# Attention block: constants filled by plan, the opening's norms in other PSUM banks, a 16-bit root for Q's norm, and another set of tie-breaks

## The chip, the cores and the metric

The kernel runs on one NeuronCore of a Trainium2 chip. A run's time is device time in microseconds. The kernel before has a median of 359.07 us over three runs (359.01 to 359.48). Times inside a run come from one profiled execution and are counted from its first instruction. The engines are TensorE (PE, matmuls), VectorE (DVE), ScalarE (ACT), GpSimd (POOL) and SyncE (SP, which issues DMAs here; ACT and POOL issue some too).

## The reference

```python
B, S, D, H = 1, 2048, 448, 16
qkv = (x @ wqkv).reshape(B, S, 3, H, Dh).transpose(2, 0, 3, 1, 4)
q, k, v = qkv[0], qkv[1], qkv[2]
scores = einsum("bhqd,bhkd->bhqk", q, k) * (Dh ** -0.5)
p = softmax(scores)
o = einsum("bhqk,bhkd->bhqd", p, v)
return o.transpose(0, 2, 1, 3).reshape(B, S, D) @ wo
```

All of x, wqkv and wo are bfloat16. A head has 28 columns. There are 16 heads of 2048 x 2048 scores, so 67 million exponentials.

## The kernel before

**Tiling.** The heads form four groups of four. A head takes 32 rows of the 128 partitions (28 columns and four rows for constants). The queries form four chunks of 512, the keys 16 tiles of 128. A set is one group with one chunk; 16 sets run one behind the other. Inside a set each head meets 16 key tiles, and one head with one tile and 512 queries is a *half*: 1024 halves in all. The scores of a half are one matmul of 32 rows (line 798), which leaves 128 keys x 512 queries in a PSUM bank.

**Two ways for an exponential.** ACT takes two halves at once from a pair of banks, `a0` or `a1`, and writes `pt` (line 1001, `do_exp`). DVE takes one half from bank `d0` or `d1`, sometimes `m` (line 1016, `do_a`). It writes the score, shifted and clipped, as an int16, whose bits read as a bfloat16 stand for a power of two (the tile `I`). Four halves make a *chain*, one `I` tile of 128 x 2048. As that power of two is only piecewise linear, each chain is used three times: as it is, and with two shifts added to the integer (`SHIFT` 43 and 85), against V, and V scaled by two weights (`VS`, `VW`). The first shift is written by DVE into a tile `J1` (line 1114, `do_add`). The second is either a second DVE write, into `J2`, or for chains that begin early in a set (`own`, set in `d_more`) an accumulating DMA that POOL issues: it adds the tile `shift2`, a constant 85, to `I` in place once the unshifted `I` has been used (line 1074, `in_place`).

**Sums.** The product with V goes to bank `o` in groups of four matmuls, one for each head (line 1176). V has a column of ones, so a set's last rows are the sums. At a set's end DVE copies `o` to `o_sb`; SP moves the sums, DVE inverts them, SP stores the result to `scr` and spreads it as `rr`, and POOL multiplies (line 1228), into `xs` or `OTL`. The output projection (line 348, bank `m`) follows.

**A bound for the softmax.** Instead of the row maximum the scores carry a bound from the norms of Q and K. For the first group it is found in the opening: `k_first` squares each K block (ACT), sums the squares by a matmul (line 452) into a bank given by its argument `nbank`, and takes the maximum on DVE (line 457). `qn_first` does the same for the first Q chunk: a matmul into a bank, an approximate square root by integer arithmetic on the bits (line 534), and the product with the root of K's largest norm (line 539), called `su`. The first scores need `su`.

**The order of the work.** One function, `plan`, writes all instructions in the order that a small planner finds. It keeps a time for each engine, gives each piece of work a duration, a priority, what it needs and what it gives, and lets the engine that is free first choose. `best` picks the ready piece of the lowest priority number. For DVE and POOL a piece can be marked `port`: then it isn't begun while the other engine is in such a piece. `after_shared` makes a POOL instruction wait for the last such DVE instruction. Small random numbers in the costs (`shake`) break ties; the plan is tried for 24 seeds, and the one with the earliest planned end is written (lines 1460 and 1461). Every engine's queue is in order.

**Outside the plan** stand the opening's loads and fills, written ahead of it. On POOL these are, in order, the identity, the cleared weights and V tiles, 14 small DMAs with constant rows for QP (line 231), then `shift2` (line 257), the float copy of the identity `identf` (line 258) and `self_`. The planner takes POOL as free from 25.6 us on. `identf` is first used in the kernel's last microseconds.

**The end.** Behind the last set's product, the projection's first three groups for each of four tiles of 128 queries are done early where PE has room (`early_jobs`); what is left of them is written by `filler` between the last steps. Then the last group follows (`OTf`), the copies (lines 1440, 1442) and the stores.

The lines that choose the seed:

```python
d = Dry()
ends = {k: plan(d, d, d, d, d, d, k, True) for k in range(NSEED)}
seed = min(ends, key=lambda k: ends[k])
```

## Time and profile before

| what | value |
|---|---|
| median of three runs | 359.07 us |
| the profiled execution's own time | 360.29 us |
| its span, first to last instruction | 358.2 us |
| busy: PE, DVE, ACT, POOL | 94%, 92%, 94%, 32% of the span |
| mean granted PE clock | 1.000 |
| exponentials on ACT | 358, from 17.27 to 349.24 us |
| halves on DVE | 278 from d, 30 from m |
| J writes on DVE | 104 |
| accumulating DMAs | 50, of 512 KB |

A row of a group of instructions has line, engine, operation, out<-in, shapes and count; then busy time and the mean of one in ns; then the idle time of the engine before them, and what ended it. A row of the timeline begins with the start and the duration in us, and has in brackets the idle time ahead of it and what ended that. A row of the chain has start, duration and what ran. In DMA queue rows (SPq, POOLq) the duration is that of the issue. Idle time counts only where the engine is the one that others wait for.

### The profile page before, as it was taken

The page shows a single profiled execution, that of the slowest core. Times are in us where ns is not written, and L with a number is a line of the kernel's source. Part 1 is how long each engine was busy: PE and PEld are TensorE (multiplying, and loading weights), DVE is VectorE, ACT ScalarE, POOL GpSimd, SP SyncE. Part 2 cuts the span into 40 slices and gives each one's busy share as a digit, 9 for nine tenths or more (in the row PEclk, how much of TensorE's full clock was granted, in tenths as well). Part 3 has the DMA queues.
Part 4 walks back from the last instruction along what each step waited for, and adds up shares of the span by engine and source line. Part 5 has one row for each costly group of instructions (what it writes and reads, how often), then busy time and mean ns, then how long its engine had stood idle before and what let it go on. Part 6 is the DMA issues. An engine that isn't in the chain of part 4 may idle for free.

```text
span 358.2 us, 11057 instructions
## 1 busy us (share of the span) xinstructions
PE 338.0 (94%) x4474; PEld 110.3 (31%) x4474; DVE 329.4 (92%) x616; ACT 338.1 (94%) x370; POOL 115.3 (32%) x164
## 2 busy tenths in 40 slices
PE   8999999999999999999989999988899899999994
PEld 4333233332234332332222222222222322222232
DVE  7789989999999899998999999999999999999933
ACT  2689999999999999999999999999999999999991
POOL 8971252413503043432223535121414131130110
PEclk9999999999999999999999999999999999999999
DMA  9430146551746437094393916464585929395211
GB/s 208 105 97 15 25 95 131 119 112 36 147 98 120 91 61 150 10 191 89 86 186 77 193 34 136 94 139 102 104 165 97 198 62 203 90 185 120 66 33 54
DMA packets 29463, 38.73 MB, mean 108 GB/s; under 512 B 15108, under 2 KB 21092, under 8 KB 29412
## 3 DMA queue, kind: packets, MB, share of 16 engines
q0 software_dynamic: 7648, 26.25, 38.5%
q1 hardware_dynamic: 20516, 11.22, 12.2%
q8 instruction: 35, 0.57, 0.7%
q10 hardware_dynamic: 1248, 0.55, 0.6%
q14 instruction: 16, 0.13, 0.1%
HBM read 6.20 MB, written 1.96 MB: 23 GB/s over the span
## 4 chain that ended last, share of the span: by engine, by line
PE 45%; ACT 37%; issue 7%; DVE 6%; DMA 3%; POOL 0%; SPq 0%; POOLq 0%; ACTq 0%; DVEq 0%
ACT pt L1001 37%; PE a L798 17%; PE o L1176 13%; PE m L341 5%; PE m L348 5%; DVE I L1016 3%; DMA scr<-rec 2%; PE o L696 1%; DVE J L1114 1%; DVE kp L457 1%; DMA rr<-scr 1%; PE d L348 1%; PE d L798 1%; PE a L341 1%; DVE V L612 0%
## 5 line engine op out<-in xcount | busy, mean ns | idle before, releaser
L1001 ACT ACTIVATE pt<-a 128x1024 bf16<-128x1024 f32 x358 | 329.5, 1167 | 3.2 <-PE d L798 1.7
L1016 DVE TENSOR_SCALAR I<-d 128x512 int16<-128x512 f32 x278 | 181.4, 680 | 9.2 <-PE d L798 8.6
L798 PE MATMUL a<-QP,KA 32*128 32x512 bf16 (+1 forms) x708 | 138.2, 380 | 11.3 <-ACT pt L1001 10.3
L1176 PE MATMUL o<-pt,V 128*32 128x512 bf16 x716 | 102.7, 383 | 0.0
L798 PE MATMUL d<-QP,KA 32*128 32x512 bf16 x275 | 95.4, 384 | 0.8 <-DVE I L1016 0.8
L798 PEld LDWEIGHTS <-KA 32*128 32x128 bf16 (+1 forms) x1035 | 48.6, 91 | 145.4 <-issue 143.7
L1074 POOL DMA_DIRECT2D I<-shift x50 | 44.0, 941 | 99.9 <-PE o L1176 28.4
L1114 DVE TENSOR_SCALAR J<-I 128x2048 int16<-128x2048 int16 x104 | 72.9, 709 | 0.7
L1176 PE MATMUL o<-I,V 128*32 128x512 bf16 x308 | 60.0, 385 | 0.0
L1176 PE MATMUL o<-J,VS 128*32 128x512 bf16 x212 | 36.0, 383 | 0.0
L1176 PEld LDWEIGHTS <-V 128*32 128x32 bf16 x1024 | 26.8, 94 | 29.8 <-issue 29.1
L1176 PE MATMUL o<-J,VW 128*32 128x512 bf16 x204 | 31.3, 384 | 0.0
L1228 POOL TENSOR_TENSOR xs<-o_sb,rr 128x512 bf16<-128x512 f32 x12 | 15.9, 1323 | 44.3 <-DMA rr<-scr 21.9
L363 POOL TENSOR_TENSOR sq<-QA 128x512 bf16<-128x512 bf16 x15 | 17.2, 1146 | 23.9 <-DVE QA L503 18.2
L363 POOL TENSOR_TENSOR sq<-KA 128x512 bf16<-128x512 bf16 x12 | 13.4, 1117 | 24.4 <-DVE KA L381 13.8
L1016 DVE TENSOR_SCALAR I<-m 128x512 int16<-128x512 f32 x30 | 20.2, 675 | 0.1
L341 PE MATMUL m<-XT,WRAW 128*32 128x512 bf16 x216 | 18.3, 386 | 0.0
L1228 POOL TENSOR_TENSOR OTL<-o_sb,rr 128x512 bf16<-128x512 f32 x3 | 3.8, 1264 | 34.4 <-DMA rr<-scr 21.7
L1176 PE MATMUL o<-I,VW 128*32 128x512 bf16 x108 | 13.7, 385 | 0.0
L348 PE MATMUL m<-WRAW,XT 128*32 128x112 bf16 (+1 forms) x432 | 13.5, 231 | 0.0
L1176 PEld LDWEIGHTS <-VS 128*32 128x32 bf16 x304 | 10.1, 94 | 9.3 <-issue 8.7
L348 PE MATMUL m<-WO,xs 128*32 128x448 bf16 x156 | 12.7, 358 | 0.0
(133 smaller groups left out, 275.8 us busy)
## 6 DMA issues: line engine op xcount, KB each, us to landing
I<-shift POOLq DMA_DIRECT2D x50, 512.0 KB, 6.0
rr<-scr SPq DMA_DIRECT2D x60, 64.0 KB
QP<-QA SPq DMA_DIRECT2D x60, 28.0 KB
out_dram<-osb SPq DMA_DIRECT2D x12, 112.0 KB
WRAW<-in_wqkv_dram SPq DMA_DIRECT2D x3, 336.0 KB
QP<-su SPq DMA_DIRECT2D x32, 2.0 KB
WO<-in_wo_dram SPq DMA_DIRECT2D x16, 24.5 KB
den<-o_sb SPq DMA_DIRECT2D x15, 8.0 KB
```

The lines of the kernel that those rows point to most:

```text
L341: nc.tensor.matmul(out=ps[HP * i:HP * (i + 1), :], lhsT=w[:, cc, h * Dh:h * Dh + HP], rhs=xt(c, cc), start=(cc == 0), stop=(cc == CC - 1), ...
L348: nc.tensor.matmul(out=out[r, :], lhsT=lhsT[:, r], rhs=rhs, start=start, stop=stop, tile_position=(0, HP * i), **k)
L363: after_shared(nc.gpsimd.tensor_tensor(out=t[:], in0=src, in1=src, op=ALU.mult))
L457: nc.vector.reduce_max(out=held["kp"][:, sc:sc + 1], in_=held.pop(nkey), axis=AX.X)
L696: nc.tensor.matmul(out=warm[:], lhsT=zero[:, 0:P], rhs=zero[:], start=True, stop=True)
L798: nc.tensor.matmul(out=out_ap, lhsT=KAt[(g, j // XB)][r, (j % XB) * P:(j % XB + 1) * P], rhs=q[r, :], start=(n == 0), stop=(n == len(terms ...
L1001: nc.scalar.activation(out=pt[:], in_=ps[:], func=ACT.Exp, scale=LN2 / 128.0)
L1016: nc.vector.tensor_scalar(out=dst, in0=pd[:], scalar1=BIAS, scalar2=0.0, op0=ALU.add, op1=ALU.max)
L1074: after_shared(nc.gpsimd.dma_start(out=ch["I"][:, w], in_=shift2[:, w], accum_op=ALU.add))
L1114: cur["shared"] = nc.vector.tensor_scalar(out=r[:, w], in0=ch["I"][:, w], scalar1=float(SHIFT[k]), scalar2=None, op0=ALU.add)
L1176: nc.tensor.matmul(out=o[HP * i:HP * (i + 1), :], lhsT=v_of(e["k"], g, j)[:, HP * i:HP * (i + 1)], rhs=e["ap"], start=(SETMM[key] == 1), s ...
L1228: m = nc.gpsimd.tensor_tensor(out=otile(g, c), in0=st["o_sb"][:], in1=st["rr"][:], op=ALU.mult)
```

## The change

Six things are changed.

- The constants. The fill of the shift tile and the cast to `identf` leave POOL's unplanned opening and become planned pieces, marked `port`: the fill as soon as the second Q chunk is in SBUF, the cast behind the fills of `WO`. Both wait for DVE's last marked instruction.
- The banks of the opening's norms: K's four norms are in o, o, a0, o, where they were in o, a0, o, a0; Q's norm is in a0, where it was in o, and has priority 2.5 for 3.15.
- The root of Q's norm is written as 16 bits (the upper half of the float's bits, read as bfloat16), where it was 32 bits. `su` reads it.
- `J1` tiles are taken when they are written, from four buffers; they were taken at the chain's start, from five. `dve_ok` no longer asks for them.
- The path by which a whole chain's first shift was accumulated into J1 (`far`) is removed; its threshold had kept it unused. In its place stands a way to accumulate both shifts (`own2`), whose threshold of 999 keeps it unused too.
- The seeds are 70 to 93, where they were 0 to 23.

Since the planner decides, all else follows: the built program has 44 accumulating DMAs (50 before), 110 J writes (104), 34 halves from bank m and 274 from d, 12 groups of filling matmuls on zeros in the main part (18), and the same 358 exponentials on ACT. The diff, cut:

```diff
-    NJ = 5
-    FAR = 99
+    NJ = 4
+    OWN2 = 999
...
+    SEED0 = 70
     NSEED = 24
...
-    shift2 = const.tile([P, HG * QW], I16, name="shift2")
-    nc.gpsimd.memset(shift2[:].bitcast(I32), SHIFT[2] * 65537)
-    nc.gpsimd.tensor_copy(out=identf[:], in_=ident[:])
+    shifts = {v: const.tile([P, HG * QW], I16, name=f"shift{v}") for v in ...}
...
             def root():
-                held["nq"] = wk.tile([P, 2 * QW], BF16, name="pt", bufs=NPT)[:].bitcast(F32)
-                nc.vector.tensor_scalar(out=held["nq"].bitcast(I32), in0=held.pop("qn0").bitcast(I32), scalar1=0.5,
-                                        scalar2=float(127 << 22), op0=ALU.mult, op1=ALU.add)
+                held["nq"] = wk.tile([P, 2 * QW], BF16, name="pt", bufs=NPT)[:, 0:QW]
+                nc.vector.tensor_scalar(out=held["nq"].bitcast(I16), in0=held.pop("qn0").bitcast(I32), scalar1=0.5 ** 17,
+                                        scalar2=float(127 << 6), op0=ALU.mult, op1=ALU.add)
...
-            add("DVE", 0.34, scaled, need=["nq0", ("km", 0)], gives=[("QA", 0, 0), "QN00"], pri=pri)
+            add("DVE", 0.27, scaled, need=["nq0", ("km", 0)], gives=[("QA", 0, 0), "QN00"], pri=pri)
...
+        def fill_shift(v):
+            after_shared(nc.gpsimd.memset(shifts[v][:].bitcast(I32), v * 65537))
+
+        def copy_ident():
+            after_shared(nc.gpsimd.tensor_copy(out=identf[:], in_=ident[:]))
+
+        for v in shifts:
+            add("POOL", 1.05, lambda v=v: fill_shift(v), need=[("Q", 0, 1)], gives=["shifts"], pri=8, port=True)
+        add("POOL", 0.8, copy_ident, need=[("QA", 0, CL)], gives=["identf"], pri=96, port=True)
...
-        k_first(1, "a1", "a0", "ACT", "ACT", 3.05, late=("ksq", 0, NQC - 1))
-        k_first(2, "d0", "o", "ACT", "ACT", 3.1, late=("ksq", 0, NQC - 1))
-        k_first(3, "d1", "a0", "DVE", "ACT", 3.2, late=("QA", 0, 0))
+        k_first(1, "a1", "o", "ACT", "ACT", 3.05, late=("ksq", 0, NQC - 1))
+        k_first(2, "d0", "a0", "ACT", "ACT", 3.1, late=("ksq", 0, NQC - 1))
+        k_first(3, "d1", "o", "DVE", "ACT", 3.2, late=("QA", 0, 0))
         q_job(0, 0, "m", QPRI, split=1)
-        qn_first("o", 3.15)
+        qn_first("a0", 2.5)
...
-                if not j1_free() or not used_up(old, 0) or any(a[0] is old for a in adds) or old["acc"] is None or old["acc"] > t:
+                if not used_up(old, 0) or any(a[0] is old for a in adds):
                     return False
...
-                    ch[1] = wk.tile([P, HG * QW], I16, name="J1", bufs=NJ)
...
-            if k == 2:
-                ch[k] = wk.tile([P, HG * QW], I16, name="J2", bufs=NCH2)
+            ch[k] = wk.tile([P, HG * QW], I16, name=f"J{k}", bufs=NJ if k == 1 else NCH2)
...
-    ends = {k: plan(d, d, d, d, d, d, k, True) for k in range(NSEED)}
+    ends = {k: plan(d, d, d, d, d, d, k, True) for k in range(SEED0, SEED0 + NSEED)}
```

More of the change, by code (lines that the diff above doesn't have):

```diff
@@ L768, in plan @@
         pts_used = [0]
[L769 removed]
+        chain = {"cur": None, "all": [], "J1": [], "J2": [], "dma": 0.0}
         a_fifo = []
@@ L898, in d_more @@
                     ch["own"] = early and rest >= FAR2
-                    if early and FAR <= rest < FAR2:
-                        ch["far"] = True
-                        far_chain(ch)
+                    ch["own2"] = early and rest >= OWN2
                 taken.append(ch["next"])
@@ L1030, in close @@
             ch["at"] = free["DVE"]
-            adds.append([ch, m, 2 if ch["far"] else 1])
+            if not ch["own2"]:
+                adds.append([ch, m, 1])
+                chain["J1"].append(ch)
             if not ch["own"]:
                 chain["J2"].append(ch)
-            if ch["far"]:
-                accumulate(ch, m)
-            elif ch["own"]:
+            if ch["own"]:
                 in_place(ch, m)
@@ L1082, in in_place @@
[L1082 to L1100 removed]
+                evt[("PV", n, 0)] = (free["PE"], "PE")
@@ new lines, in line, with emit, landed @@
+            def line(k, need):
+                def emit():
+                    by = SHIFT[k] if not ch["own2"] else SHIFT[k] - SHIFT[k - 1]
+                    after_shared(nc.gpsimd.dma_start(out=ch["I"][:, w], in_=shifts[by][:, w], accum_op=ALU.add))
+                def landed(end):
+                    at = landing(end)
+                    for q in range(m):
+                        pending.append({"step": ch["steps"][q], "k": k, "ap": ch["I"][:, q * QW:(q + 1) * QW].bitcast(BF16),
+                                        "ready": at, "pt": None, "ch": ch})
+                add("POOL", 0.88, emit, need=need + ["shifts"], gives=[("own", n, k)], pri=9, port=True)
+                ops["POOL"][-1].after = landed
```

54 lines of the change are left out of this document (13 added, 41 removed).

## The prediction

> **What bounds the kernel now.** I read the busy table of the page first, then the busy time in stretches, then the ScalarE (ACT) timeline, then what ended its idle time.
>
> ```profile
> PE 338.0 (94%) x4474; PEld 110.3 (31%) x4474; DVE 329.4 (92%) x616; ACT 338.1 (94%) x370; POOL 115.3 (32%) x164
> 33.00:110.00 77.00, 75.54 (x1134) 25.20 (x1134) 73.51 (x130) 76.88 (x85) 23.24 (x26) 1.00 0.43 89
> ```
> The second line is one of the stretches: 77 us, with the busy time of PE, weight loads, DVE, ACT and POOL, then the clock (1.00), the DMA share and GB/s. PE, DVE and ACT are all nearly full there, ACT most (76.88 of 77).
>
> ```profile
> 41.06 0.70 ACT pt L1001
> 48.29 0.73 ACT pt L1001
> 17.27 1.94 ACT L1001 ACTIVATE pt<-a 128x1024 bf16<-128x1024 f32 x2 [0.79 <-PE a L798]
> 26.13 54.48 ACT L1001 ACTIVATE pt<-a 128x1024 bf16<-128x1024 f32 x59 [0.89 <-PE d L798]
> L1001 ACT ACTIVATE pt<-a 128x1024 bf16<-128x1024 f32 x358 | 329.5, 1167 | 3.2 <-PE d L798 1.7 <-PE a L798 0.8 <-PE o L1176 0.5
> ```
> The chain shows the exponentials of 41.06 and 48.29 eight steps apart: 7.23/8 = 0.904 us for one. 358 of them fill 323.6 us. The first starts at 17.27, the last ends at 349.24 (333.55 + 15.69, a row below): 332.0 us, so 8.4 us are lost between them, and 9.0 us follow. Both programs list 358 exponentials and 308 halves on VectorE (DVE). So the time is: first exponential + 323.6 + losses + end. Only these can move.
>
> **The change, part by part.**
>
> *Opening, norms and root.* DVE's serial tail of the opening:
>
> ```profile
> 10.72 0.38 PE L830 MATMUL d<-zero 128*128 128x512 bf16 x1
> 11.16 0.83 PE L341 MATMUL d<-XT,o_sb 128*32 128x512 bf16 x12
> 13.17 0.68 DVE L534 TENSOR_SCALAR pt<-o 128x512 int32<-128x512 int32 x1
> 14.57 0.38 PE L452 MATMUL a<-sq,blockK 128*128 128x512 bf16 x1
> 14.98 0.69 DVE L457 TENSOR_REDUCE kp<-a 128x1 f32<-128x512 f32 x1
> 16.09 0.49 DVE L539 TENSOR_SCALAR su<-pt,kroot 128x512 bf16<-128x512 f32 x1
> 16.63 0.39 PE a L798 x2
> 17.21 0.48 DVE L631 TENSOR_SCALAR VS<-V 128x512 bf16<-128x512 bf16 x2
> ```
> Q's norm now runs in bank a0 where the filler of 10.72 stood, and the root goes ahead of the second maximum. The last maximum (14.98) still waits for K3's square and norm (14.57). What comes before it gains at most the 0.44 us between the filler and K2's projection (11.16), and nothing at least; as the norm takes the filler's slot, I take a small part, 0.08. The root is still read from PSUM: its 0.6 us stays, off the path. `su` stands between the last maximum and the first scores (16.09, 0.49; scores at 16.63). With a 16-bit input its nearest row is VS, 16 bits to 16 bits: two in 0.48, so 0.24. Gain 0.25. If the pointer scalar kept it slow it would be 0; the whole of 0.49 is the other bound. Sum **-0.33**.
>
> *The constants.* They are fills and casts on GpSimd (POOL), unplanned now:
>
> ```profile
> 14.69 8.00 POOL L231 DMA_DIRECT2D QP<-offs  x14
> 22.15 0.53 POOL L231 DMA_DIRECT2D QP<-offs  x1
> 22.30 1.91 DVE L1114 TENSOR_SCALAR J<-I 128x2048 int16<-128x2048 int16 x1
> 22.68 0.97 POOL L257 MEMSET shift<- 128x1024 int32 x1
> 23.58 0.77 POOL L258 CAST identf<-ident 128x128 f32<-128x128 bf16 x1
> 24.85 0.37 PE L798 MATMUL d<-QP,KA 32*128 32x512 bf16 x1 [0.81 <-DVE I L1016]
> L1114 DVE TENSOR_SCALAR J<-I 128x2048 int16<-128x2048 int16 x104 | 72.9, 709 | 0.7
> 28.81 1.04 POOL L363 TENSOR_TENSOR sq<-QA 128x512 bf16<-128x512 bf16 x1 [4.16 <-DVE QA L503]
> 34.47 1.07 SPq L572 DMA_DIRECT2D QP<-su  x2
> ```
> The J write that meets `shift` and `identf` takes 1.91 us where the mean is 0.71: 1.2 more. The next I then frees its bank late, PE stands 0.81 in its queue at the d matmul of 24.85, and ACT idles 0.89 before 26.13. With the fill moved behind Q(0,1)'s evacuation this J runs free. Between none and the whole 1.2, I take **-0.9**, the ACT gap itself. DVE is late next: it has no gap until 33. What moves: the fill (0.97) now stands ahead of the square of 28.81 (1.04), so the rows of QP1 (34.47) come about 1 us later against the exponentials. By the lists their first user is exponential 22, due at 17.27 + 22 x 0.904 = 37.2 at the earliest, 2.7 us after 34.47; covered with some 1.7 left. `identf` (0.77) goes behind the WO fills on POOL, 32% busy; nothing, and its 0.77 if an accumulation waited for it.
>
> *Accumulations and J writes.* The lists have 44 accumulating DMAs for 50 and 110 J writes for 104. POOL's issues cost nothing (32% busy). DVE gets six times 0.60 = 3.6 us (two J take 1.20 in the chain, below).
>
> ```profile
> 29.92 1.20 DVE J L1114 x2
> DVE I L1016 <- PE d L798: 8.6, 25, 1.1
> 349.79 0.75 DVE L1417 COPY pt<-o 128x256 f32<-128x256 f32 x2 [6.16 <-PE o L1176]
> ```
> DVE waits 8.6 us for score matmuls, and 6.16 us before the last copy. These hide the 3.6: **0**, and up to 3.6 without that cover (a rival). The J1 buffers (five to four, taken at the write instead of at the chain's start) cost nothing while J is read in time: J's idle is 0.7 over 104.
>
> *The other order of the middle.* Tie-breaks differ, so gaps come and go. Two gaps near the end have a cause that the lists let me follow:
>
> ```profile
> 313.21 2.63 POOL L1074 DMA_DIRECT2D I<-shift  x3
> 317.89 0.85 POOL L1074 DMA_DIRECT2D I<-shift  x1 [2.04 <-PE o L1176]
> 319.25 8.66 DMA scr<-rec
> 327.63 0.40 PE L1176 MATMUL o<-I,VS 128*32 128x512 bf16 x4 [0.44 <-DMA I<-shift]
> 332.76 0.37 PE L348 MATMUL m<-WO,OTL 128*32 128x448 bf16 x4 [0.57 <-POOL OTL L1228]
> 333.55 15.69 ACT L1001 ACTIVATE pt<-a 128x1024 bf16<-128x1024 f32 x17 [0.41 <-PE d L798]
> ```
> Three accumulations pile up behind OTL1's product and leave at 313.21 together; the fourth (317.89) lands when PE has stood 0.44 for it. The store of 1/sum (319.25) takes 8.66 us behind them, OTL2 is late, PE stands 0.57. Together 1.0. In the new list three accumulations stand between OTL1 and OTL2, not four, the first of them later. Gain between 0 and 1.0; other gaps of this kind may come, so half: **-0.5**.
>
> PE works in groups of four matmuls between scores. Three groups between two scores are more than a step holds:
>
> ```profile
> 88.39 0.76 PE o L1176 x12
> 98.47 0.55 PE o L1176 x8
> ```
> The third adds 0.21. After the opening the new list has 33 such steps for 29. Four times 0.21 is 0.84 at most; the second score bank hides part, and ACT idled only 0.5 on `o` in all; I take **+0.25**. The fillers on zeros fall from 18 to 12 groups: idle PE time, 0.
>
> *The end.* Behind the last product the new list has more output-projection groups left: two into m and three into a0, where now there is one, into a0.
>
> ```profile
> 352.44 0.56 PE L348 MATMUL d<-WO,OTf 128*32 128x448 bf16 x8
> 352.88 0.37 PE L348 MATMUL m<-WO,OTf 128*32 128x448 bf16 x4
> 353.08 0.36 PE L348 MATMUL a<-WO,xs 128*32 128x448 bf16 x4
> 353.27 0.36 PE L348 MATMUL a<-WO,OTf 128*32 128x448 bf16 x4
> 353.75 0.62 DVE L1440 CAST pt<-a 128x448 bf16<-128x448 f32 x1
> ```
> A group takes 0.19 (353.08 to 353.27). Four more, 0.76, less 0.05 of gap before 352.88: the last group starts at 353.98 and ends 0.36 later, so the cast starts at 354.38, not 353.75: **+0.65** on the end. Nothing later hides it; only groups done earlier would (0).
>
> Sum: -0.33 - 0.9 + 0 - 0.5 + 0.25 + 0.65 = **-0.83 us**. The span of 358.2 becomes 357.4, the profiled execution's 360.29 becomes 359.46. That execution lies 1.22 above the median of the runs, so I carry the difference over: 359.07 - 0.83 = **358.24**, told as 358.2.
>
> **A rule against it.** Row: the J began at 22.30, the fill at 22.68, and J is the one that took 1.91. The Trainium skill, "SBUF — State Buffer", section "Who interferes with whom", says that DVE in a two-port mode and GpSimd exclude each other for a whole instruction, and that issue order decides who blocks. By that, read from these starts, J would have held the port, and the fill would not have cost DVE anything. The trace does not agree, unless the descriptor work of 22.15, which started first and stays in the program, was what stopped J; then the sum without the gain is 358.24 + 0.9 = 359.1.
>
> **Rivals.**
>
> *The stretch of J stays.* POOL's issue of 22.15 (0.53) is under way when J starts, and is unmoved. If it was what held J, or if the fill meets another J at 28, the 0.9 is not gained: 359.14. For it: J starts inside that issue. Against: VS at 21.18 or 17.21 (0.48 for two) is not stretched although POOL issues such DMAs from 14.69 to 22.68. Chance 0.22.
>
> *DVE becomes the bound (slower).* Place: the I behind a J write. Each J that stands before an I whose bank PE waits for costs 0.60, as 24.85 shows for a long one. At the end the last scores for DVE stand three exponentials before the last, now nine; DVE's 6.16 of slack shrinks by 6 x 0.904 and gains the 0.53 of an output copy that moves ahead: 1.3 left. It decides once DVE runs more than 1.3 late, or once its 8.6 of waiting is used up by fixed waits. Four of six J's on the path: 358.24 + 2.4 = 360.6. For it: DVE at 92%. Against: the 8.6 us, and the J's prices equal those in the planner. Chance 0.20.
>
> *More is gained.* The rest of the two late gaps goes (another 0.5) and the end's groups find room (0.65): 357.1. Chance 0.11.
>
> **How the numbers follow.** My own sum has 0.47, with 357.2 to 359.0 about it, since the gaps of a new order are known to some 0.8 only. What a measurement tells from no change is about 0.2%, 0.72 us: faster is below 358.35, slower above 359.79. Faster: 0.38 of my 0.47 and the 0.11, 0.49. Same: 0.08 of mine and 0.18 of the first rival, 0.26. Slower: 0.20, 0.01 of mine and 0.04 of the first rival with a dear middle: 0.25. The range takes in the lower rival's middle and the dear one's: 356.7 to 360.8.
>
> **What would show it.** `su` near 0.25 and the first exponential near 16.95; the second J after it near 0.7 and no gap of 0.9 about 25; POOL's fill at about 27 to 28 with no J beside it. At the end, the last cast 0.65 later after the last exponential. Wrong would be: DVE's waits for d far below 8.6 with ACT idle behind I; a stretched J in the first 40 us; or gaps of 0.5 in the middle that sum to over 8.

## The result and the profile after

The changed kernel takes 357.18 us in the median (356.71 to 358.38), the kernel before 359.22 beside it (358.90 to 359.79). The ratio is 0.9941, 95% interval 0.9926 to 0.9956: 2.04 us less, between 1.6 and 2.7. The forecast was 358.2 with a range of 356.7 to 360.8. The sign and the range hold; the gain is 2.5 times the 0.83 that the sum gave, and the terms of the sum didn't come out as they were sized.

The profiled execution of the changed kernel took 358.38 us with a span of 355.7, against 360.29 and 358.2: 2.5 us of span. First the busy line, one of the stretches (the one shown in the prediction, with the same columns), then from the groups of lines ScalarE's exponentials and VectorE's J writes:

```profile
PE 335.3 (94%) x4449; PEld 110.4 (31%) x4449; DVE 331.9 (93%) x622; ACT 337.8 (95%) x370; POOL 110.6 (31%) x158
33.00:110.00 77.00, 75.55 (x1141) 25.38 (x1140) 72.59 (x127) 77.00 (x85) 21.75 (x25) 1.00 0.38 79
L1005 ACT ACTIVATE pt<-a 128x1024 bf16<-128x1024 f32 x358 | 329.1, 1165 | 1.3 <-PE a L805 0.7 <-PE d L805 0.4 <-PE m L805 0.2
L1095 DVE TENSOR_SCALAR J<-I 128x2048 int16<-128x2048 int16 x110 | 75.6, 699 | 0.6
```

ScalarE is still the engine that is full. It idles 1.3 us ahead of its 358 exponentials, where it idled 3.2, and 77.00 of 77 us are busy in the stretch that had 76.88. VectorE has 2.5 us more work (331.9 for 329.4); its J writes alone are 2.7 more (75.6 for 72.9). TensorE's granted clock is 1.00 in that stretch in both.

Where the 2.5 us of span went, by the starts of ScalarE's exponentials in the two executions (both have 358; the n-th need not be of the same half in both, as VectorE's shares differ):

| stretch | before | after | difference |
|---|---|---|---|
| start to the first projection matmul | 7.79 | 7.44 | -0.35 |
| from there to the first exponential | 9.48 | 9.25 | -0.23 |
| 1st to 34th exponential | 31.92 | 30.51 | -1.41 |
| 34th to 156th | 111.73 | 111.90 | +0.17 |
| 156th to 166th | 10.17 | 9.42 | -0.74 |
| 166th to 321st | 142.26 | 143.05 | +0.79 |
| 321st to the end of the last | 35.89 | 34.96 | -0.93 |
| last exponential to the end of the span | 9.00 | 9.21 | +0.21 |

The sum is -2.50 (the rows are rounded). The rows behind it, of the changed kernel's timeline, from the opening and the first stretch (start, duration; in brackets the idle time ahead):

```profile
7.44 1.05 PE L339 MATMUL a<-XA,o_sb 128*32 128x512 bf16 x16
15.64 0.35 DVE L537 TENSOR_SCALAR su<-pt,kroot 128x512 bf16<-128x512 bf16 x1
16.69 1.94 ACT L1005 ACTIVATE pt<-a 128x1024 bf16<-128x1024 f32 x2 [0.66 <-PE a L805]
18.81 15.00 ACT L1005 ACTIVATE pt<-a 128x1024 bf16<-128x1024 f32 x16 [0.19 <-PE d L805]
21.71 0.69 DVE L1095 TENSOR_SCALAR J<-I 128x2048 int16<-128x2048 int16 x1
19.87 3.17 POOL L231 DMA_DIRECT2D QP<-offs  x5
25.20 0.95 POOL L708 MEMSET shift<- 128x1024 int32 x1 [1.78 <-DVE VS L629]
```

`su` takes 0.35 for 0.49. The J of 21.71 takes 0.69 where its counterpart took 1.91, although GpSimd issues DMAs from 19.87 to 23.04 (the issue that J meets, at 21.56, takes 0.94 where its neighbours take 0.54 to 0.57); the fill comes at 25.20, not at 27 to 28 as forecast, and with no J beside it. ScalarE has no gap behind 18.81.

The stretch at 156 is one that the prediction did not price. The kernel before on VectorE and ScalarE, and then the changed one on VectorE:

```profile
161.42 0.69 DVE L503 CAST QA<-m 128x512 bf16<-128x512 f32 x1 [0.72 <-PE m L341]
162.03 1.28 DVE L1016 TENSOR_SCALAR I<-d 128x512 int16<-128x512 f32 x2
162.48 3.77 ACT L1001 ACTIVATE pt<-a 128x1024 bf16<-128x1024 f32 x4 [0.27 <-PE o L1176]
```

```profile
159.61 1.28 DVE L1095 TENSOR_SCALAR J<-I 128x2048 int16<-128x2048 int16 x2
160.81 0.68 DVE L501 CAST QA<-m 128x512 bf16<-128x512 f32 x1
161.41 1.28 DVE L1020 TENSOR_SCALAR I<-d 128x512 int16<-128x512 f32 x2
```

Before, VectorE reaches the cast of a Q chunk 0.72 us ahead of its projection, and two score banks stand behind that wait; the exponential of 162.48 comes 0.66 late. In the new order two J writes stand ahead of the cast, and nothing waits. This is the order's doing and no accident of one execution: the part from the 156th to the 166th takes 10.17 in all six traces with before's order (before and five of the runs below), and 9.28 to 9.43 in the five with the changed one's.

Near the end the accumulations now leave one by one, and ScalarE runs 27 exponentials from 321.52 without a gap (GpSimd's rows, then ScalarE's):

```profile
310.20 0.88 POOL L1067 DMA_DIRECT2D I<-shift  x1 [3.72 <-PE o L1157]
312.33 0.86 POOL L1067 DMA_DIRECT2D I<-shift  x1 [1.25 <-PE d L805]
315.91 0.86 POOL L1067 DMA_DIRECT2D I<-shift  x1 [2.73 <-PE o L1157]
321.52 25.01 ACT L1005 ACTIVATE pt<-a 128x1024 bf16<-128x1024 f32 x27
```

And one new loss, in the stretch from the 166th to the 321st (VectorE, GpSimd, then ScalarE):

```profile
243.03 2.97 DVE L1095 TENSOR_SCALAR J<-I 128x2048 int16<-128x2048 int16 x3
244.01 1.45 POOL L1209 TENSOR_TENSOR xs<-o_sb,rr 128x512 bf16<-128x512 f32 x1 [2.77 <-DMA rr<-scr]
247.78 4.86 ACT L1005 ACTIVATE pt<-a 128x1024 bf16<-128x1024 f32 x5 [0.22 <-PE d L805]
```

Three J writes take 2.97, where three take about 1.9: the third, at 244.24, takes 1.76 because GpSimd multiplies a set by its reciprocals at 244.01.

### The profile page after: what moved, and what is told of

Same layout as the page of the kernel before. It is cut to its first block, busy times and chain, and to the rows that moved or that the text cites. A ratio compares the mean times of both kernels' runs of the same rounds, so it can differ in the third digit from the quotient of the medians.

```text
span 355.7 us, 10990 instructions
## 1 busy us (share of the span) xinstructions
PE 335.3 (94%) x4449; PEld 110.4 (31%) x4449; DVE 331.9 (93%) x622; ACT 337.8 (95%) x370; POOL 110.6 (31%) x158
## 4 chain that ended last, share of the span: by engine, by line
ACT 52%; PE 34%; issue 8%; DVE 4%; DVEq 0%
ACT pt L1005 52%; PE a L805 12%; PE o L1157 9%; PE m L339 5%; PE m L346 3%; DVE I L1020 2%; PE o L694 1%; DVE J L1095 1%; PE d L339 1%; PE a L339 1%; PE m L837 1%; PE o L837 0%; DVE QA L501 0%; PE d L346 0%; PE d L676 0%
## 5 line engine op out<-in xcount | busy, mean ns | idle before, releaser
L1157 PE MATMUL o<-pt,V 128*32 128x512 bf16 x716 | 104.2, 383 | 0.1
L805 PE MATMUL d<-QP,KA 32*128 32x512 bf16 (+1 forms) x271 | 94.6, 384 | 0.2 <-DVE I L1020 0.2
L1095 DVE TENSOR_SCALAR J<-I 128x2048 int16<-128x2048 int16 x110 | 75.6, 699 | 0.6
L1067 POOL DMA_DIRECT2D I<-shift x44 | 39.3, 905 | 96.2 <-PE o L1157 26.9
L1157 PE MATMUL o<-I,V 128*32 128x512 bf16 x308 | 65.2, 384 | 0.7 <-DVE o_sb L1186 0.5
L1157 PE MATMUL o<-J,VW 128*32 128x512 bf16 x232 | 37.5, 384 | 0.0
L1157 PE MATMUL o<-J,VS 128*32 128x512 bf16 x208 | 31.9, 382 | 0.0
L1020 DVE TENSOR_SCALAR I<-m 128x512 int16<-128x512 f32 x34 | 23.1, 680 | 0.0
L1157 PEld LDWEIGHTS <-VW 128*32 128x32 bf16 x328 | 10.5, 94 | 10.6 <-issue 9.5
L805 PE MATMUL m<-QP,KA 32*128 32x512 bf16 (+1 forms) x34 | 13.0, 384 | 0.5 <-DVE I L1020 0.5
```

Source lines behind the costliest of these rows:

```text
L805: nc.tensor.matmul(out=out_ap, lhsT=KAt[(g, j // XB)][r, (j % XB) * P:(j % XB + 1) * P], rhs=q[r, :], start=(n == 0), stop=(n == len(terms ...
L1020: nc.vector.tensor_scalar(out=dst, in0=pd[:], scalar1=BIAS, scalar2=0.0, op0=ALU.add, op1=ALU.max)
L1067: after_shared(nc.gpsimd.dma_start(out=ch["I"][:, w], in_=shifts[by][:, w], accum_op=ALU.add))
L1095: cur["shared"] = nc.vector.tensor_scalar(out=r[:, w], in0=ch["I"][:, w], scalar1=float(SHIFT[k]), scalar2=None, op0=ALU.add)
L1157: nc.tensor.matmul(out=o[HP * i:HP * (i + 1), :], lhsT=v_of(e["k"], g, j)[:, HP * i:HP * (i + 1)], rhs=e["ap"], start=(SETMM[key] == 1), s ...
```

## The experiments

Times are medians; ratios are to the kernel before, with their 95% intervals. "Stretch" means, unless said otherwise, that from the first exponential to the 34th: 31.92 before, 30.51 after.

**The constants moved, in the order of before.**

```diff
-    nc.gpsimd.memset(shift2[:].bitcast(I32), SHIFT[2] * 65537)
-    nc.gpsimd.tensor_copy(out=identf[:], in_=ident[:])
...
+                if (g, b, k) == (0, 2, 2):
+                    after_shared(nc.gpsimd.memset(shift2[:].bitcast(I32), SHIFT[2] * 65537))
...
+            if gg == G - 1:
+                after_shared(nc.gpsimd.tensor_copy(out=identf[:], in_=ident[:]))
```

> The kernel before, with every other instruction in its place: POOL's fill of the second shift's constant is given out behind the second piece of VS of block 2 (it becomes the shared work before the third), and POOL's cast of the identity behind the last fill of the output projection's zeros. The outputs are the reference's. My theory: it was POOL's fill that stretched J at 22.30 to 1.91 us; with the fill elsewhere that J takes about 0.70, ScalarE's gap of 0.89 before the ninth exponential goes, and the gain is carried to the end: 358.1 to 358.3 us, ratio about 0.997. Rival (the stretch stays, because POOL's descriptor writing or something else stretched J): J still takes 1.2 to 1.9 and the time is 359.1, ratio 1.000. Second rival (the gain is eaten on the way, by a later wait that was already there): the ninth exponential comes 0.9 earlier, the last one less than 0.3 earlier.

Measured: 358.86, ratio 0.999 (0.9975 to 1.0006). The J's of the opening are free (0.69 and 0.68), and the stretch takes 30.73, 1.2 less than in the profiled execution of before. But the time falls by only 0.3 to 0.4, and the interval reaches no change. My theory holds in the trace and not in the size. The second rival has a part in this execution: the exponentials are 0.76 early at the first (an earlier start), 1.95 to 1.97 from the 17th to the 241st and 1.24 at the last. Of what is lost again 0.33 comes behind J writes at 242.65 and 267.95, which took 1.77 and 1.17 beside GpSimd (before: 1.13 at 244.62), and 0.40 behind the 321st exponential. But another part counts for the median: the kernel before doesn't always lose as much in its opening as its profile shows. In two of three other runs with that opening it lost 0.9 to 1.1 less.

**When the fill meets a J.** Two runs told of below, on the root and on the stores, and the one with small late DMAs leave the opening's constants where before had them. VectorE and GpSimd with the small late DMAs:

```profile
22.40 0.69 DVE L1116 TENSOR_SCALAR J<-I 128x2048 int16<-128x2048 int16 x1
23.86 0.97 POOL L257 MEMSET shift<- 128x1024 int32 x1
```

and with the small stores:

```profile
22.18 1.85 DVE L1114 TENSOR_SCALAR J<-I 128x2048 int16<-128x2048 int16 x1
22.51 0.97 POOL L257 MEMSET shift<- 128x1024 int32 x1
```

The same program up to there, the same J; GpSimd gets to its fill between 22.5 and 23.9, as its 14 small DMAs go, and that decides. The stretch took 30.81 in the first and 31.88 in the second. It is a toss in each execution, and the one shown as "before" had drawn the dear side (and a late start: its first projection matmul is at 7.79, others of that kernel's opening are between 6.75 and 7.88). That fits its own time, 1.2 above the median; the execution with the small stores lay 1.1 above the median of its kernel. How often the dear side falls isn't measured. Of the 88 executions of the kernel before that were timed beside the runs below, 14 took 360.0 us or more and the rest at most 359.85; which of them had the collision isn't known, but if it is those, it falls about once in six.

**The constants put back, in the new order.**

```diff
+    for v in shifts:
+        nc.gpsimd.memset(shifts[v][:].bitcast(I32), v * 65537)
+    nc.gpsimd.tensor_copy(out=identf[:], in_=ident[:])
...
-            after_shared(nc.gpsimd.memset(shifts[v][:].bitcast(I32), v * 65537))
+            pass
```

> The changed kernel with the same order of all other work, but POOL's two fills of constants and its cast of the identity put back into its opening, as before; the planned pieces are left empty. The outputs are the reference's. My theory: the J that is written while POOL fills is stretched again to 1.5 to 2 us and the ninth exponential comes 0.9 to 1.0 later than in the changed kernel; carried to the end this makes 358.1 us, ratio to the kernel before 0.997 against 0.994 for the changed kernel. Rival (the order of the ties alone brought it): J stays at 0.7 and the time stays at 357.2, ratio 0.994.

Measured: 357.69, ratio 0.9947 (0.9928 to 0.9966), 0.2 us above the changed kernel's ratio and inside its interval. In the profile the fill came at 23.26 and the J of 23.62 took 1.16; the stretch took 30.97, 0.46 more than 30.51. So the direction is my theory's and the price is less than half of it.

**The fill twice.** To meet a J in every execution:

```diff
     nc.gpsimd.memset(shift2[:].bitcast(I32), SHIFT[2] * 65537)
+    nc.gpsimd.memset(shift2[:].bitcast(I32), SHIFT[2] * 65537)
```

> The kernel before with one instruction more: POOL's fill of the shift constant (0.97 us) stands there twice, one behind the other. The outputs are the reference's. Four executions of kernels with the fill in the opening show what it costs DVE to depend on when POOL reaches it: at 22.68 the J of 22.30 took 1.91 us (the profiled run of before), at 23.14 the J of 23.81 took 0.85, at 23.26 the J of 23.62 took 1.16, and at 23.86 no J took over 0.69. My theory now: the fill stretches J whenever the two overlap, and in the usual execution of before they overlap little, which is why moving the fill away was worth only 0.1%. Two fills cover about 23.2 to 25.1, where the second J stands in every execution: that J takes 1.6 to 2.0 and the time rises by 0.7 to 1.0 over the kernel before, 360.0, ratio 1.002 to 1.003. Rival (the fill does not hold J; the 1.91 was an accident of that one execution): J stays under 0.9 and the time at 359.2, ratio 1.000.

Measured: 359.81, ratio 1.0015 (1.0001 to 1.0030), 0.5 us more, less than the 0.7 to 1.0 that I expected.

```profile
24.24 1.51 DVE L1115 TENSOR_SCALAR J<-I 128x2048 int16<-128x2048 int16 x1
23.22 0.97 POOL L257 MEMSET shift<- 128x1024 int32 x1
24.25 0.95 POOL L258 MEMSET shift<- 128x1024 int32 x1
```

The J took 1.51 and the stretch 31.64. It is the fill that holds J: the rival, that 1.91 was an accident, falls. A second fill makes the kernel 0.5 dearer, and moving the fill away 0.35 cheaper, the latter not apart from no change: so the median of before carries at most a part of the 1.1 to 1.2 that its profile shows.

**The 16-bit root alone.**

```diff
-                held["nq"] = wk.tile([P, 2 * QW], BF16, name="pt", bufs=NPT)[:].bitcast(F32)
-                nc.vector.tensor_scalar(out=held["nq"].bitcast(I32), in0=held.pop("qn0").bitcast(I32), scalar1=0.5,
-                                        scalar2=float(127 << 22), op0=ALU.mult, op1=ALU.add)
+                held["nq"] = wk.tile([P, 2 * QW], BF16, name="pt", bufs=NPT)[:, 0:QW]
+                nc.vector.tensor_scalar(out=held["nq"].bitcast(I16), in0=held.pop("qn0").bitcast(I32), scalar1=0.5 ** 17,
+                                        scalar2=float(127 << 6), op0=ALU.mult, op1=ALU.add)
```

> The kernel before with an identical order on every engine; only the root of Q's first norm is written in 16 bits instead of 32. The outputs are the reference's within its tolerance. My theory: the product su that reads it takes about 0.35 instead of 0.49 us, the first exponential starts 0.15 to 0.25 us earlier, and all that follows with it: 358.9 to 359.1, ratio 0.9993 to 0.9996. Rival: the first exponential comes earlier, but the collision of POOL's fill with J (22.30) takes the gain back or adds to it, because it shifts the one against the other: the last exponential moves by less than 0.05 or by more than 0.4.

Measured: 359.08, ratio 0.9997 (0.9984 to 1.0009), which alone doesn't tell a gain from none; `su` takes 0.36. An execution's first exponential can't be read against another's, since the start of the projections moves by a microsecond. From the first projection matmul to the first exponential it takes 9.36, where the kernel before takes 9.48 (and 9.48 or 9.49 in three other runs with its opening): 0.12 to 0.13 less. The changed kernel takes 9.25, and 9.23 to 9.25 in five of the runs that have its opening. The other 0.11 is left for the norms' banks, which no run takes alone. (In three runs, with projections from 6.75, 6.76 and 7.06 on, it takes 0.25 to 0.6 longer than in others of their kind.)

**The late DMAs made small.** On the kernel before:

```diff
+                cur["nacc"] = cur.get("nacc", 0) + 1
+                v = w if cur["nacc"] <= 46 else slice(0, QW // 8)
-                after_shared(nc.gpsimd.dma_start(out=ch["I"][:, w], in_=shift2[:, w], accum_op=ALU.add))
+                after_shared(nc.gpsimd.dma_start(out=ch["I"][:, v], in_=shift2[:, v], accum_op=ALU.add))
```

> The kernel before with the same instructions; of its 50 accumulating DMAs the last four (the 47th to the 50th) move 64 of 2048 columns each instead of all. It leaves out the second shift of the remaining columns of these four, so their exponentials are wrong in those columns, while the work of every engine is unchanged. My theory: the burst of accumulations at 313.2 and 317.9 held up the store behind them (8.66 us) and the chunk's last DMA; without it both late gaps of ScalarE (0.44 before 327.63 and 0.57 before 332.76) go and the last exponential comes 0.8 to 1.0 earlier, ratio 0.997. The value that I took in the sum was half of that, 0.5, ratio 0.9986. Rival (the gaps come from the order of the engines and not from the queue): both gaps stay, ratio 1.000.

Measured: 358.43, ratio 0.9982 (0.9967 to 0.9997), 0.65 us less, somewhat under the 0.8 to 1.0 expected. SyncE and ScalarE:

```profile
318.28 0.33 SPq L1221 DMA_DIRECT2D scr<-rec  x1
321.85 1.72 SPq L1227 DMA_DIRECT2D rr<-scr  x4
321.57 15.91 ACT L1001 ACTIVATE pt<-a 128x1024 bf16<-128x1024 f32 x17
```

The spread of `rr` is issued 3.6 us after the store of `scr`; it was 8.7. ScalarE has no pause of 0.2 us or more, and the part from the 321st exponential to the last takes 35.23 instead of 35.89 (36.09 to 36.29 in four other traces with before's order). The burst did cause the late gaps. In the changed kernel, with its accumulations one by one, the same part takes 34.96 (34.96 to 35.02 in five traces): at least the whole 0.93 that I had halved.

**Twelve J writes more.** On the changed kernel:

```diff
+            cur["nadd"] = cur.get("nadd", 0) + 1
+            if cur["nadd"] % 9 == 4:
+                x = wk.tile([P, HG * QW], I16, name="JX", bufs=1)
+                cur["shared"] = nc.vector.tensor_scalar(out=x[:, w], in0=ch["I"][:, w], scalar1=float(SHIFT[k]), scalar2=None, op0=ALU.add)
```

> The changed kernel with twelve J writes more (each ninth one is followed by a second one of the same size into a spare tile that nobody reads): 12 x 0.60 = 7.2 us more on DVE, twice what the six J writes of the change added. The outputs are the reference's. My theory in the prediction: such work hides in DVE's waits for score matmuls (8.5 us) and ahead of the last copy; then the time rises by less than 1 us, to 357.2 to 358.2, ratio 0.994 to 0.997. Rival (DVE is the bound: each J stands before an I whose bank TensorE waits for): each costs its 0.60, and the time is 364.4, ratio 1.014. In between, the ratio tells what share of such a write lies on the path.

Measured: 359.80, ratio 1.001 (0.9998 to 1.0022), 2.5 us above the changed kernel: 0.21 for each, a third of its 0.60. What hides is visible in VectorE's waits, first the changed kernel's, then this one's (us, times, longest):

```profile
DVE I L1020 <- PE d L805: 8.5, 21, 1.1
DVE pt L1398 <- PE o L1157: 2.5, 1, 2.5
```

```profile
DVE I L1020 <- PE d L805: 6.5, 16, 1.1
DVE pt L1402 <- PE o L1161: 2.4, 1, 2.4
```

Of 7.2 us only 2.0 went into the waits for scores and nothing into the wait before the last copy. Both theories are wrong: VectorE isn't the bound, but its waits take up only a part of the work that is added. The price is a rough one: by the two intervals it lies between 0.13 and 0.29 for each; in the trace the last exponential ends 1.75 us later after the first, and 0.67 more is lost behind the last cast, at the stores. Also, GpSimd's pieces that wait for VectorE's last marked instruction now wait for the added writes as well, and what of the 2.5 comes by that way wasn't taken apart.

**The product behind the J writes.** In the changed kernel, the product of 244.01:

```diff
+                def emit():
+                    after_shared(nc.gpsimd.tensor_tensor(out=otile(g, c), in0=st["o_sb"][:], in1=st["rr"][:], op=ALU.mult))
+                if s == 8 and cur["nadd"] < 71:
+                    cur["late"] = emit
+                else:
+                    emit()
...
+            if cur["nadd"] == 71 and "late" in cur:
+                cur.pop("late")()
```

> The changed kernel with one instruction moved: POOL's product of the ninth set with the spread reciprocal (244.01, 1.45 us) is given out behind the third of the three J writes that DVE makes at 243.03, instead of ahead of them. The outputs are the reference's. My theory: the J of 244.24 that took 1.76 us takes 0.69, the gaps of ScalarE at 246.4, 247.8 and 251.6 (0.43, 0.18 and 0.34) go, and the last exponential comes 0.7 to 1.0 earlier than in the changed kernel: 356.2 to 356.5, ratio to the kernel before 0.9915 to 0.992. Rival (the product is late then, and so are the rows of the next set, for there is one buffer for them): the gaps move to the product of 250.72 and the time stays at 357.2, ratio 0.994.

Measured: 357.32, ratio 0.9942 (0.9926 to 0.9958): no gain. Yet the trace does what the theory says:

```profile
242.61 1.89 DVE L1095 TENSOR_SCALAR J<-I 128x2048 int16<-128x2048 int16 x3
244.58 1.26 POOL L1213 TENSOR_TENSOR xs<-o_sb,rr 128x512 bf16<-128x512 f32 x1 [3.77 <-DVE J L1095]
237.69 18.61 ACT L1005 ACTIVATE pt<-a 128x1024 bf16<-128x1024 f32 x20
```

Three J's take 1.89, ScalarE has no gap, and from the 166th to the 321st exponential it takes 142.26 for 143.05. But the run without the end's groups, next, has the old product and takes 142.26 as well: its J's there were not met. There the product came at 241.34, when its DMA had landed, and the J's at 242.75. This, too, is a toss of the execution, and the median doesn't show it.

**Four groups of the output projection taken out at the end.**

```diff
-                op.emit()
+                if n < XB * G or op.gives[0][2] == 0:
+                    op.emit()
```

> The changed kernel without four of the output-projection groups behind the last product (two of the three into the bank m and two of the three into a0), so that one group is left to either bank. It leaves out three quarters of the last projections of those rows, and the output differs there. My theory: each group takes TensorE 0.19 us behind the last product, so the last cast starts 0.65 to 0.75 earlier and the time is 356.5, ratio to the kernel before 0.992. Rival (something else sets the last cast, the copy of the product or the cast ahead of it on DVE): it comes less than 0.2 earlier, and the time stays at 357.1, ratio 0.994.

Measured: 356.89, ratio 0.9926 (0.9911 to 0.9940), 0.5 us below the changed kernel's ratio, with intervals that overlap. The last cast, of the changed kernel and of this one:

```profile
351.74 0.62 DVE L1421 CAST pt<-a 128x448 bf16<-128x448 f32 x1 [0.70 <-PE a L346]
```

```profile
349.97 0.62 DVE L1422 CAST pt<-a 128x448 bf16<-128x448 f32 x1
```

It starts 5.21 us after the last exponential's end with the groups (346.53 to 351.74) and 4.51 without (345.46 to 349.97), as in the kernel before (349.24 to 353.75): 0.70, forecast 0.65. But from that cast to the end of the span it is 4.00 with them and 4.53 without, 4.49 before. Of 0.70 only 0.2 reaches the end in this pair of executions. (It is not always so: of four traces with these groups two took 3.98 and 4.00 there, and two, the runs with the constants put back and with twelve J writes more, 4.56 and 4.67.) The share of time in which the DMA engines are busy, between 351.5 and 357 in slices of 0.14 us, before and after:

```profile
DMA  0000040000000000000000039999999997000000
```

```profile
DMA  0001999999962992000000000000200000000000
```

Before, the three last stores (224, 112 and 112 KB) run as one block; after, the third comes behind a dip.

**The first two of the last stores made small.** On the kernel before:

```diff
                 if hf == 1:
-                    (nc.sync if k else nc.scalar).dma_start(out=out_at(c, tq), in_=osb[:, k, :])
+                    w = P if k else 8
+                    (nc.sync if k else nc.scalar).dma_start(out=out_at(c, tq)[0:w], in_=osb[0:w, k, :])
             if hf == 0:
-                nc.sync.dma_start(out=out_at(c, 0, 2), in_=osb)
+                nc.sync.dma_start(out=out_at(c, 0, 2)[0:8], in_=osb[0:8])
```

> The kernel before, but of the last chunk's three stores the first two (224 and 112 KB) write 8 of 128 rows each; 120 of 128 rows of three quarters of that chunk are left out of the output. All work of the engines is the same. Seen so far: with four groups more at the end the last cast came 0.70 later after the last exponential (as forecast), but the program ended only 0.2 later, for the time from the start of that cast to the end of the span fell from 4.49 to 4.00. My theory: in the kernel before the last store shares the DMA engines with the two others, and the later one of the changed kernel has them for itself. Then the span here ends about 4.0 after the start of the last cast, and the time falls by 0.5: 358.7, ratio 0.9986. Rival (the last store's time has nothing to do with the others): 4.5, ratio 1.000.

Measured: 358.80, ratio 0.9983 (0.9970 to 0.9996), 0.6 us less. The last cast and the busy DMA engines (the window of above):

```profile
353.84 0.62 DVE L1440 CAST pt<-a 128x448 bf16<-128x448 f32 x1
DMA  0000004000000000000000022201894000000000
```

The span ends 3.92 after the start of the last cast, which stands 4.51 behind the last exponential as before. So the two other stores do hold up the last one, and by the amount forecast. Whether they do it in the DMA engines or in SyncE's queue, which issues the 224 KB store ahead of the last, wasn't taken apart. That a later last store finds the way free holds for two of the four traces above.

**The tie-breaks.** Three runs with other seeds; the changed lines are `SEED0 = 0` and `SEED0 = 200` in the changed kernel, and `range(70, 70 + NSEED)` in the kernel before.

> The changed kernel with the tie-breaks of the kernel before (0 to 23 instead of 70 to 93); everything else of the change stays. The outputs are the reference's. The planner gives the chosen order 345.51 us, against 345.38 for that of the changed kernel. My theory: the opening (-0.3) and the constants (-0.35) stay, the late gaps and the gap at 160.9 are matters of the order and come out anew: anywhere between 356.5 and 359, ratio 0.9925 to 0.9995. Rival one (the tie-breaks brought all but 0.65 of the gain): ratio about 0.998. Rival two (the tie-breaks are worth what the planner says, 0.1 us): 357.3, ratio 0.9945.

> The kernel before with the tie-breaks of the changed one (70 to 93 instead of 0 to 23) and nothing else changed. The outputs are the reference's. The planner gives the chosen order 344.59 us, against 345.37 for that of the kernel before: 0.78 less. If the planner's figures hold on the chip: 358.4, ratio 0.998. My theory (an order has its own collisions and late transfers, which the planner doesn't see, and the one of before has 0.66 at 160.9 and 1.15 near the end): between 357.5 and 359.2, ratio 0.995 to 1.000. Rival (the set of tie-breaks does nothing): ratio 1.000.

> The changed kernel with the tie-breaks 200 to 223, among which the planner finds the shortest order of 240: 344.03 us, 1.36 less than the order of the changed kernel. The outputs are the reference's. If the planner's figures hold on the chip: 355.8, ratio 0.990. My theory (what the planner doesn't see is of the same size as what it ranks): between 355.8 and 358, ratio 0.990 to 0.997. Rival (the planner's ranking says nothing): ratio 0.994 or worse.

| kernel | seeds | planned, us | time, us | ratio |
|---|---|---|---|---|
| before | 0 to 23 | 345.37 | 359.2 | 1 |
| before | 70 to 93 | 344.59 | 357.96 | 0.9961 (0.9942 to 0.9980) |
| changed | 0 to 23 | 345.51 | 359.78 | 1.0011 (0.9996 to 1.0025) |
| changed | 70 to 93 | 345.38 | 357.18 | 0.9941 (0.9926 to 0.9956) |
| changed | 200 to 223 | 344.03 | 359.97 | 1.0006 (0.9991 to 1.0022) |

The draws also share the work out anew: with 70 to 93 in the kernel before, and with 200 to 223, ScalarE makes 356 exponentials and VectorE 312 halves, for 358 and 308 in the three others. Two exponentials are 1.8 us of ScalarE, by the 0.904 of the prediction; the one kernel gained 1.4 and the other nothing.

With the old seeds the changed kernel gains nothing, although it has the better opening (9.23 from the first projection matmul to the first exponential) and a free J (the stretch takes 30.72). It gives nearly all back between the 34th and the 156th exponential: 114.16 us against 111.90. There stand stalls of VectorE and TensorE:

```profile
84.84 0.40 PE L346 MATMUL m<-sq,maskK 128*32 128x512 bf16 x4 [1.10 <-POOL sq L361]
97.66 0.29 DVE L563 TENSOR_SCALAR su<-z 128x512 int16<-128x512 int16 x1 [1.79 <-DMA QP<-su]
98.60 0.37 PE L805 MATMUL d<-QP,KA 32*128 32x512 bf16 x1 [1.17 <-DVE I L1020]
```

A norm's matmul waits 1.10 for GpSimd's square; `su` waits 1.79 for an earlier DMA and holds the I behind it. The planner's figure doesn't foresee them: it put this order 0.13 behind the other, and the chip puts it 2.6 behind. The order that it liked best of 240, 1.35 ahead of the changed kernel's, is as slow as this one (1.0006 and 1.0011, with intervals that overlap). So for the old seeds all three expectations fall, my range too, which ended at 0.9995. The kernel before with the new seeds comes out inside my range. For the seeds from 200 on the rival holds: among these five the planner's ranking says nothing.

## Why the prediction was right, and where it was wrong

That the kernel gets faster held, for the change as a whole. The steps:

- **Opening, -0.33.** Measured -0.23: the root gives 0.12 to 0.13, not 0.25, since `su` takes 0.35 and not the 0.24 of VS; what is left for the norms' banks is 0.11, where I took 0.08. What looked like 0.58 in the traces (17.27 to 16.69) is for 0.35 an earlier start of the projections, no part of the change.
- **Constants, -0.9.** The mechanism was right: the fill stretches J, moving it frees J, and ScalarE's gap goes. The price was taken from one execution in which it had happened in full, and charged to the median. The runs that isolate it give 0.35 (moved alone) and 0.2 (put back), neither apart from 0 by its interval; profiles with before's opening show the stretch between 30.81 and 31.92. So the term that failed is this one's size: I carried "the difference" of one execution over to the median, but a collision that an execution may or may not have is not carried over in full. The rival "the stretch of J stays" falls: with the fill elsewhere J took 0.69, though GpSimd was issuing a DMA when it began.
- **Accumulations and J writes, 0.** Twelve J's more cost 0.21 each, so "hidden" was too good: an estimate by that price is 6 x 0.21 = 1.3, though the planned order had placed these six and the twelve were put in behind it. What the six cost in the changed kernel was not measured by itself, so what this term should have been stays open. The cover I named was not the one: the wait before the last copy (6.16 before, 2.52 now) shrank by the new order and took up none of the twelve.
- **Late gaps, -0.5.** The cause was right, as the small DMAs show, and halving it was wrong: this part is 0.93 shorter, and by the other traces of before's order up to 1.3.
- **Three-group steps, +0.25.** The stretch from the 34th to the 156th, in which no other gap is told of, is 0.17 longer. That agrees, but what of it is this and what J writes stays open.
- **The end, +0.65.** The last cast comes 0.70 later, as worked out; the program's end 0.2 later in the profiled pair, 0.5 by the ratios of the run without the groups. The step that failed is "nothing later hides it": the stores do, in part, in two of four traces.
- **What wasn't in the sum** is the 0.74 around 161, a wait that before's trace shows and that I left to "other gaps may come". With the late gaps it makes 1.67 of the gain, and both are matters of the order.

So of about 2.0 us some 0.6 comes, by these sizes, from the opening and the constants (0.23 and 0.35, the second not apart from nothing), and the rest from which order the seeds drew. That split is an estimate: every change of the program makes a seed draw another order, so no run parts the draw cleanly from the rest. By themselves, the new seeds gave the kernel before 1.4 us, and the change with the old seeds gave nothing. That my sum of -0.83 came as near as it did was luck: the constants were credited with too much, while the middle was credited with too little and the end charged too hard. The rival that VectorE becomes the bound falls (its waits for scores are 8.5, as before); "more is gained", 357.1 with 0.11, named the right time: the late gaps went in full, as it said, and the end's groups found no room but were covered in part by the stores.

The rule of the Trainium skill that the prediction set against the trace, in "SBUF — State Buffer", section "Who interferes with whom", has two halves. That the loser blocks fully agrees: in the eight collisions of the table below, J ends 0.54 to 0.56 us after GpSimd's instruction does, however early it began; and of the 61 J writes that took 0.76 us or more in all fourteen traces, 59 end 0.55 to 0.56 after a fill, square or product of GpSimd. That issue order decides can't be read off the recorded starts in the opening: J began 0.38 ahead of the fill (22.30 and 22.68), 0.33 (22.18 and 22.51) and 0.12 (24.03 and 24.15, in the kernel before with the new seeds), and lost each time. But in all three a DMA issue of GpSimd was already under way when J began, and ran up to the fill. Where none was, a J that began 0.2 to 0.4 ahead of a product kept its 0.69, and the product waited. So it is in the changed kernel, with the second of the three J's, at 243.63, and the product of 244.01 (1.45 for 1.26); and in the changed kernel with the old seeds:

```profile
122.32 0.69 DVE L1095 TENSOR_SCALAR J<-I 128x2048 int16<-128x2048 int16 x1
122.53 1.61 POOL L1209 TENSOR_TENSOR xs<-o_sb,rr 128x512 bf16<-128x512 f32 x1 [6.80 <-DMA rr<-scr]
```

These agree with the rule. That the prediction's trace spoke against it is therefore not shown. An issue alone doesn't hold J, as the 0.69 of 21.71 shows, and in two traces a J kept its 0.70 although an issue was under way and a fill came 0.2 after it began (47.27 with the old seeds, 47.52 with those from 200 on). Why the fill won in the opening stays open. The eight collisions:

| J start | took | GpSimd's instruction | ended | J's end after it |
|---|---|---|---|---|
| 22.30 | 1.91 | fill, 22.68 | 23.65 | 0.56 |
| 22.18 | 1.85 | fill, 22.51 | 23.48 | 0.55 |
| 24.03 | 1.64 | fill, 24.15 | 25.12 | 0.55 |
| 24.24 | 1.51 | second fill, 24.25 | 25.20 | 0.55 |
| 23.62 | 1.16 | fill, 23.26 | 24.23 | 0.55 |
| 23.81 | 0.85 | fill, 23.14 | 24.11 | 0.55 |
| 244.24 | 1.76 | product, 244.01 | 245.46 | 0.54 |
| 244.21 | 1.79 | product, 244.18 | 245.45 | 0.55 |

## What to carry to other kernels

Before a stall of one profiled execution is priced into the median, ask what times it: if it starts with a DMA's landing, it is a toss, and its worth is its price times how often it falls. When a planner's order changes with the edit, the order can be the larger edit: here five draws of ties lay between 357.2 and 360.0 us, while the parts that were meant to help gave some 0.6, and the planner's own figure did not rank them; so try other draws first, and keep an order because it was measured. A group of work added ahead of the last store may not be paid in full where that store would have queued behind others.

## What the runs showed that was not expected

- A 2-byte J write that is held by a fill or a product of GpSimd ends 0.55 us after GpSimd's instruction, whether it was recorded as starting 0.38 before it or 0.67 within it. A DMA issue of GpSimd alone did not do this: J took 0.69, and the issue 0.94 for 0.54.
- The start of the projections moves by 1.1 us between executions (6.75 to 7.88), and with it the 16 transposes ahead of it (in four traces from 5.04 or 5.56, 1.06 to 1.75 long); why is open. Of the two earliest starts (6.75 and 6.76) 0.29 and 0.25 was not kept.
- A small store behind four accumulating DMAs of 512 KB held up the load that follows it by 5 us (8.7 from issue to issue, 3.6 with four of these DMAs cut to 64 of 2048 columns).
- With the two stores ahead of it cut to 8 of 128 rows, the last store ends the span 3.92 us after the start of its cast, and 4.49 with them in full: 0.57, close to what four groups of the output projection add (0.70).
